# Third combination in the staging tiles, late rows' subtraction tied three products behind their load, last sums made as soon as they are whole

## The chip, the cores and the metric

The kernel runs on one core of one Trainium2 chip. The metric is the device time of one execution in microseconds (us).

## What is computed

The inputs are float32: 2048 rows `x` of width 576, a key and a value cache of 16 heads with 2048 positions, weights, and a conditioning vector `c`. The reference, cut to what matters:

```
mod = silu(c) @ w_mod                      # six vectors of width 576: sa, ca, ga, sb, cb, gb
h = layernorm(x) * (1 + ca) + sa
q = h @ wq                                 # 32 heads of 128; keys/values: 16 heads, last 512 positions
x = x + ga * (softmax(q k^T / sqrt(128)) v) @ wo
h = layernorm(x) * (1 + cb) + sb
x = x + gb * ((sigmoid(h @ w_gate) * (h @ w_up)) @ w_down)     # inner width 4608
```

## The kernel before

**Two stages.** The 2048 rows are four blocks of 512, and a block is four tiles t = 0..3 of 128 rows. Attention runs first, up to about 1801 us. The change touches only the second stage, the gated layer: gate and up products, sigmoid, product, down product.

**Seven products.** Blocks are taken in pairs, pair 0 (blocks 0 and 1) and then pair 1 (blocks 2 and 3, "late rows"). For each pair the step number u runs over 36 slices of the inner width (u = 0..71 in all). A two-by-two matrix product is formed with seven products in place of eight, so each u has seven products A11, A12, S1, S2, S4, S3 and A22 (A22 of u stands behind A11 of u+1). One `product` is seven matmuls (L1087), out of a PSUM tile a, b or c, from a combination `hc` of the pair's normalized rows (seven combinations, c = 0..6) and a weight tile `sw`. Behind each product `load_w` issues one more weight load (L941); ten tiles rotate, so that load stands ten products ahead of its use.

**Combinations.** `combo_parts` makes one combination: 12 transposes on PE (L915) from a staged copy, copies on ScalarE (L918), subtractions on VectorE (L920, L923). In u = 0, product c makes combination c + 2 between its own matmuls. Staged copies come from DRAM (`scr`). For pair 0, combinations 0 to 2 are loaded early into three "rooms" of a large tile, `xp0`. One more is staged in two small tiles tagged "ts" (`stage`, L894). The other three are loaded by `stage_room` (L901) into rooms that have been read: two of them between weight loads 6 and 7 ahead of the first product, one behind the first product. All loads are issued on SyncE (SP in the profile), in order.

**Late rows.** Pair 1's rows are normalized during pair 0. `late_tile(t)` loads two tiles h0, h1 (`h<-xscr`, L1147), subtracts the mean and scales on VectorE (L1152), goes on with GpSimd (L1153, L1154 and three differences), and stores pieces to `scr` (L1161, L1162). It is a generator: `late_some` takes one step behind each product, and pins what the step yields, so it keeps its place in program order. A step that yields `None` only lets one product go by. What is not pinned is placed by a scheduler, which writes each engine's order ahead of time.

**Down products and sums.** `down` makes one of seven partial results (L255, three matmuls into PSUM tile w, of which there are four) and VectorE adds it to an accumulator ACC (L1028; L1026 for the first). 28 downs belong to a group of two u. At the end of a pair, `finish_steps(t)` puts the seven accumulators together: for each t four sums on VectorE (L1011, L1012, L1014, L1016) and four on GpSimd (L1013, L1015, L1017, L1018). The last group of the kernel, GL, is done another way: `open_gl` and `close_gl` (matmuls L1035, L1036, L1043; VectorE L1045) add straight into the four output parts and store them.

In pair 0 the sums stand where the last down of each t is. In pair 1 they wait in a list: before each first down of A11 in the last group four sums are taken from it and pinned (`finish_some(4)`), and one part of the last group goes to `x22`, which the sums read:

```
            if g == GL:
                if a[0] == A11:
                    finish_some(4)
                open_gl(*a, t)
                continue
```

Other VectorE lines named below: L1245 (gate and up for A22), L1282, L1293 (sums ahead of the sigmoids), L1297 and L1300 (v1, ahead of the down products), L977 (low half of `hl`, the down products' left side; its high half is ScalarE's L976).

Of the kernel before, what the change touches and what calls it, by code (L numbers as in the profile page):

```python
# [13 lines left out]
OP = mybir.AluOpType  # L14
# [4 lines left out]
TPB = BLK // P  # L19
# [5 lines left out]
def adaln_block_kernel(ctx: ExitStack, tc: tile.TileContext, x, k_cache, v_cache, wq, wo, w_gate, w_up, w_down,  # L25
                       c, w_mod, out):
    nc = tc.nc
# [53 lines left out]
    def pin(i):  # L81
        tc.keep_in_program_order(i)
# [66 lines left out]
    xp = [const.tile([P, 2, TPB, D], F32, tag=f"xp{h}", name=f"xp{h}") for h in range(2)]  # L149
# [508 lines left out]
    D3 = 3 * P  # L658
# [52 lines left out]
    A11, A12, S1, S2, S4, S3, A22, A21 = range(8)  # L711
# [132 lines left out]
    for n in range(NLO, N + 2 * TPB):  # L844
# [8 lines left out]
        b, i = divmod(n, TPB)  # L853
# [31 lines left out]
    NG = NF // 2  # L885
# [10 lines left out]
        STG[pair, c] = halves  # L896

    def stage_room(c):
        v = xp[0].rearrange("p b t d -> p (b t d)")[:, (c - 3) * TPB * D3 : (c - 2) * TPB * D3]
        v = v.rearrange("p (t d) -> p t d", t=TPB)  # L900
        pin(nc.sync.dma_start(v, scr[0][c]))  # L901
        STG[0, c] = [v[:, 0:2], v[:, 2:4]]
# [46 lines left out]
    ORDER = (A11, S3, A22, S1, A12, S2, S4)  # L949
    WITH = {A11: 0, A12: 1, S1: 2, S2: 3, S4: 6, S3: 4, A22: 5}  # L950
    HL, VAL, SD = {}, {}, {}
    ACC = {}
    for k, a in enumerate(ORDER):
        ACC[a] = bg_view(k // 2, (k % 2) * TPB * D2, [TPB, D2])
    x22 = bg_view(3, TPB * D2, [TPB, D2])

    GL = 2 * NG - 1
# [24 lines left out]
        (nc.gpsimd.tensor_add if op == "+" else nc.gpsimd.tensor_sub)(v, VAL[g, x0], VAL[g, x1])  # L982
        VAL[g, a] = v

    todo, to_finish, X22 = [], [], -1

    def init_acc(pair):
        b0, b1 = 2 * pair, 2 * pair + 1
# [5 lines left out]
        nc.sync.dma_start(of[2 * pair + i][:, t, n0 : n0 + D2], ACC[a][:, t, :])  # L994

    def finish(pair, t):
        for _ in finish_ops(pair, t):
            pass
        if pair == 0:
            for a in (A12, A22, S4, S1):  # L1000
                store_out(a, pair, t)

    def finish_ops(pair, t):
        for i in finish_steps(t):
            if pair:
                pin(i)
            yield i

    def finish_steps(t):
        c = {a: ACC[a][:, t, :] for a in ORDER}  # L1010
        yield nc.vector.tensor_add(c[A12], c[A12], c[A11])  # L1011
        yield nc.vector.tensor_add(c[S2], c[S2], c[A11])  # L1012
        yield nc.gpsimd.tensor_add(c[S4], c[S4], c[S1])  # L1013
        yield nc.vector.tensor_add(c[S3], c[S3], c[S2])  # L1014
        yield nc.gpsimd.tensor_add(c[S1], c[S1], x22[:, t, :])  # L1015
        yield nc.vector.tensor_add(c[A22], c[A22], c[S3])  # L1016
        yield nc.gpsimd.tensor_add(c[S4], c[S4], c[S2])  # L1017
        yield nc.gpsimd.tensor_add(c[S1], c[S1], c[S3])  # L1018

    def down(a, t, hl, w, fresh):  # L1020
        cols = slice(t * P, (t + 1) * P)
# [19 lines left out]
    def close_gl():  # L1041
        p, lo_l, w, val_, to, t = half_done.pop(0)
        nc.tensor.matmul(p, lo_l, w, start=False, stop=True)  # L1043
        acc = x22[:, t, :] if to == X22 else ACC[to][:, t, :]
        nc.vector.tensor_add(acc, p, acc)  # L1045
        if val_ in (A12, A22):
            store_out(to, 1, t)

    def finish_some(k):
        while k and to_finish:  # L1050
            if next(to_finish[0], X22) == X22:
                to_finish.pop(0)
            else:
                k -= 1

    def down_some(k):
        for _ in range(k):
            if not todo:
                return
            g, a, t = todo.pop(0)  # L1060
            if g == GL:
                if a[0] == A11:
                    finish_some(4)
                open_gl(*a, t)
                continue
            down(a, t, HL[g, a], SD[g, a], g % NG == 0 and a in (S3, A11, S1, S2))
            if t == TPB - 1:
                load_sd()
            if a == ORDER[-1] and g == GL - 1:
                to_finish.append(finish_ops(1, t))  # L1070
            elif a == ORDER[-1] and g % NG == NG - 1:
                finish(g // NG, t)

    parts = []
# [67 lines left out]
    def late_tile(t):  # L1142
        lo, hi = slice(0, D2), slice(D2, D)
        h0, h1, ts_ = [fh.tile([P, 2, D3], F32, tag="ts", name=n, bufs=3).rearrange("p a d -> p (a d)")[:, :D]
                       for n in ("h0", "h1", "tt")]
        for i, h in enumerate((h0, h1)):
            nc.sync.dma_start(h, xscr[HB + i][:, t, :])  # L1147
        for _ in range(2):
            yield None
        for i, h in enumerate((h0, h1)):  # L1150
            mv, y = LN[HB + i]
            nc.vector.tensor_scalar(h, h, mv[:, t, 0:1], y[:, t : t + 1], op0=OP.subtract, op1=OP.mult)  # L1152
            yield nc.gpsimd.tensor_mul(h, h, rows2["scale"])  # L1153
            yield nc.gpsimd.tensor_add(h, h, rows2["shift"])  # L1154

        def put(c, v):
            puts.append([2, c, v])

        def put_now(c, v):
            d = scr[1][c][:, t, :]  # L1160
            nc.sync.dma_start(d[:, 0:D2], v)  # L1161
            nc.sync.dma_start(d[:, 2 * P + TQ : 2 * P + 4 * TQ].rearrange("p (q d) -> p q d", q=3),  # L1162
                              v[:, None, 2 * P :].to_broadcast([P, 3, TQ]))

        put_fn[0] = put_now
        put(0, h0[:, lo])
        yield nc.gpsimd.tensor_sub(ts_[:, lo], h1[:, lo], h0[:, lo])
        put(1, h0[:, hi])
        put(2, ts_[:, lo])
        yield nc.gpsimd.tensor_sub(ts_[:, hi], h1[:, hi], ts_[:, lo])  # L1170
        put(3, ts_[:, hi])
        put(4, h1[:, hi])
        yield nc.gpsimd.tensor_sub(h1[:, lo], h1[:, hi], h1[:, lo])
        put(5, h1[:, lo])
        yield nc.gpsimd.tensor_sub(h0[:, lo], h0[:, hi], ts_[:, hi])
        put(6, h0[:, lo])
        for _ in range(4):
            yield None
        assert not puts
# [7 lines left out]

    for c_ in first_ts:
        STG[0, c_] = first_ts[c_]
    stage(0, 6)  # L1190
    for c_ in range(2):
        load_combo(0, c_)
    for n_ in range(10):
        if n_ == 6:
            for c_ in (3, 4):
                stage_room(c_)
        load_w()

# [7 lines left out]
    for u in range(U + 1):  # L1206
# [8 lines left out]
        def swap(c, to):  # L1215
            if u == 0:
                if c == 0:
                    stage_room(5)
                if c in (T2, B22):
                    park_x(HB + c - T2)  # L1220
            if to:
                load_combo(to, c)
                if c + 2 < 7:
                    stage(to, c + 2)
# [8 lines left out]
        if u > 0:  # L1233
            v, qa = back
            g = (u - 1) // 2
            if u == U:
                finish_some(99)
                pd = fpsum("b", 1, [P, BLK])
                product(u - 1, A22, T4, pd, True, (1, 3, 5))
                nc.vector.tensor_add(u3, pd, u3)  # L1240
                nc.vector.tensor_mul(v, u3, v)
            else:
                product(u - 1, A22, T4, qa, False, (1, 3, 5) if u >= U - 1 else (2, 5))
                swap(T4, pair if u % NF == 0 else None)
                nc.vector.tensor_mul(v, qa, v)  # L1245
            if g == GL:
                a, ops = (A11, ((0, A12), (7, S4))) if u % 2 else (A12, ((1, A12), (6, S4)))
                VAL[g, a] = v
                split_val(g, a)
                todo += [(g, (a, o, to), t) for t in range(TPB) for o, to in ops]  # L1250
            elif u % 2:
                VAL[g, A11] = v
                split_val(g, A11)
                sum_val(g, S3, "-", A11, A21)
                later.append((g, S3))
            else:
                VAL[g, A12] = v
                split_val(g, A12)
                sum_val(g, S4, "-", A12, S2)
                later += [(g, a) for a in (S1, S2, S4) if (g, a) not in HL]  # L1260
                if g == GL - 1:
                    split_later()
                    todo += [(g, a, t) for a in ORDER[:2] for t in range(TPB)]
                    todo += [(g, a, t) for t in range(TPB) for a in ORDER[2:]]
                elif g % NG == NG - 1:
                    todo += [(g, a, t) for a in ORDER[:3] for t in range(TPB)]
                    todo += [(g, a, t) for t in range(TPB) for a in ORDER[3:]]
                else:
                    todo += [(g, a, t) for a in ORDER for t in range(TPB)]
# [30 lines left out]
        nc.vector.tensor_mul(v1, v1, g1)  # L1300
        g = u // 2
        if g == GL:
            a, ops = (A22, ((1, A22), (6, S1))) if u % 2 else (A21, ((0, A22), (7, X22)))
            VAL[g, a] = v1
            split_val(g, a)
            todo += [(g, (a, o, to), t) for t in range(TPB) for o, to in ops]
        elif u % 2 == 0:
            VAL[g, A21] = v1
        else:
            VAL[g, A22] = v1  # L1310
            split_val(g, A22)
            sum_val(g, S1, "+", A21, A22)
            if g == GL - 1:
                split_val(g, S1)
            sum_val(g, S2, "-", S1, A11)
            if g == GL - 1:
                split_val(g, S2)
# [29 lines left out]
```

## Time and profile before

| | us |
|---|---|
| median of 3 runs | 3071.37 (3070.59 to 3075.82) |
| the profiled execution's own time | 3071.1 |
| its span in the trace | 3069.3 |
| mean granted TensorE clock | 0.998 |
| PE busy in the span | 3039.1 |

The span is what the trace covers; the time also has 1.8 us around it. PE is busy for 99% of the span. In 40 slices of it PE's busy share is 90% or more in all but the last one, where it is 80 to 90%. Times in microseconds from the span's start place a row in the program: the second stage begins at about 1801, the late rows are normalized up to about 1990, pair 0 ends at about 2450, and the last group of down products begins at about 3030.

### The profile page before, as it was taken

Reading aid. Unit: us, or ns where it says so; the run is one execution under the profiler, and the core shown is the slowest. Engines: PE = TensorE matmul, PEld = TensorE weight load, DVE = VectorE, ACT = ScalarE, POOL = GpSimd, SP = SyncE. Lnnn points to the kernel's source line nnn. Section 1 sums busy time; section 2 is a strip of 40 time slices with the busy share of each in tenths; the row PEclk is TensorE's granted clock in tenths of the full one; section 3 lists DMA queues with packets and bytes.
Section 4 is the critical chain, followed back from the end, with each engine's and each line's share of the span. In section 5 each row is a group of like instructions: output and inputs, shape, how many; then the busy total and the mean of one; then the engine's idle time right before and its main releaser. Section 6 shows DMA issues by size and latency. Waiting matters only on the chain.

```text
span 3069.3 us, 48908 instructions
## 1 busy us (share of the span) xinstructions
PE 3039.1 (99%) x16959; PEld 2635.6 (86%) x16959; DVE 2135.9 (70%) x4145; ACT 1419.7 (46%) x2834; POOL 1487.6 (48%) x1584
## 2 busy tenths in 40 slices
PE   9999999999999999999999999999999999999998
PEld 7888888888888888888888878888888888888887
DVE  7777777777888777777777776555555665555557
ACT  5666656565555555555555543222332323322322
POOL 2656655556334445655555416633444354444433
PEclk9999999999999999999999999999999999999999
DMA  5666766666313346544454458776666676666663
GB/s 165 181 190 177 202 168 170 192 168 190 110 60 96 93 126 163 138 128 134 121 138 127 134 189 267 251 222 197 198 198 199 220 256 198 199 199 198 197 198 109
DMA packets 567841, 526.74 MB, mean 172 GB/s; under 512 B 180518, under 2 KB 443690, under 8 KB 566826
## 3 DMA queue, kind: packets, MB, share of 16 engines
q1 hardware_dynamic: 567584, 523.60, 57.9%
q8 instruction: 135, 2.21, 0.3%
q14 instruction: 112, 0.92, 0.1%
q10 hardware_dynamic: 10, 0.00, 0.0%
HBM read 366.22 MB, written 157.25 MB: 171 GB/s over the span
## 4 chain that ended last, share of the span: by engine, by line
PE 94%; DVE 3%; DMA 2%; issue 0%; ACT 0%; POOL 0%; SPq 0%; DVEq 0%; POOLq 0%; ACTq 0%
PE a L1087 14%; PE wo L255 13%; PE qp L255 13%; PE w L255 12%; PE ot L255 12%; PE st L255 11%; PE st L426 7%; PE c L1087 7%; PE b L1087 4%; PE w L915 1%; DMA h<-xscr 0%; DMA wm<-in_w_mod_dram 0%; DMA sw<-wsc 0%; DVE xp L1014 0%; DMA xp<-scr 0%
## 5 line engine op out<-in xcount | busy, mean ns | idle before, releaser
L1028 DVE TENSOR_TENSOR xp<-w,xp 128x288 f32<-128x288 f32 x948 | 431.8, 457 | 466.2 <-PE w L255 461.2
L255 PE MATMUL wo<-wb,ov 128*128 128x288 f32 x3060 | 615.2, 308 | 0.9 <-DVE ov L444 0.5
L429 ACT ACTIVATE ptt<-st 128x512 fp32r<-128x512 f32 x512 | 306.7, 599 | 635.5 <-PE st L426 635.3
L1087 PE MATMUL a<-hc,sw 128*128 128x512 f32 x2009 | 584.5, 395 | 4.5 <-DVE v L1297 4.4
L255 PEld LDWEIGHTS w<-sd,hl 128*128 128x128 f32 x2940 | 498.3, 188 | 85.2 <-DVE xp L1026 0.9
L459 DVE SCALAR_TENSOR_TENSOR xp<-wo,rs,xp 128x288 f32<-128x288 f32 x1020 | 511.4, 512 | 55.8 <-PE wo L255 6.2
L408 DVE TENSOR_REDUCE neg<-st 128x1 f32<-128x512 f32 x512 | 352.2, 688 | 279.9 <-PE st L255 278.9
L255 PE MATMUL w<-sd,hl 128*128 128x288 f32 x2940 | 546.4, 294 | 0.5 <-DVE xp L1026 0.5
L255 PEld LDWEIGHTS wo<-wb,ov 128*128 128x128 f32 x3060 | 480.4, 189 | 46.6 <-DVE ov L444 0.9
L255 PE MATMUL ot<-ptt,vs 128*128 128x512 f32 x1536 | 441.2, 394 | 0.1
L255 PE MATMUL qp<-hTm,wa 128*128 128x512 f32 x1536 | 438.6, 394 | 1.8 <-DVE qt L388 1.8
L255 PE MATMUL st<-kt,qt 128*128 128x512 f32 x1535 | 434.3, 391 | 0.2 <-DVE ptt L430 0.2
L1087 PEld LDWEIGHTS a<-hc,sw 128*128 128x128 f32 x2009 | 353.3, 188 | 45.5 <-DVE v L1297 6.5
L794 POOL TENSOR_TENSOR xp<-xp 128x896 fp32r<-128x896 f32 (+2 forms) x135 | 260.5, 1929 | 248.8 <-ACT xp L789 246.3
L414 ACT ACTIVATE pp<-st,neg 128x512 f32<-128x512 f32 x512 | 351.3, 686 | 51.3 <-DVE neg L408 49.0
L430 DVE TENSOR_TENSOR ptt<-st,ptt 128x512 fp32r<-128x512 f32 x512 | 348.3, 680 | 4.1 <-ACT ptt L429 3.7
L255 PEld LDWEIGHTS st<-kt,qt 128*128 128x128 f32 x1535 | 287.5, 188 | 60.6 <-DVE ptt L430 0.7
L426 PEld LDWEIGHTS st<-ident,pp 128*128 128x128 f32 x2048 | 253.4, 139 | 67.3 <-ACT pp L414 2.0
L426 PE MATMUL st<-ident,pp 128*128 128x128 f32 x2048 | 306.3, 272 | 0.5 <-ACT pp L414 0.4
L1087 PE MATMUL c<-hc,sw 128*128 128x512 f32 x1008 | 306.3, 395 | 0.1
L255 PEld LDWEIGHTS qp<-hTm,wa 128*128 128x128 f32 x1536 | 260.9, 188 | 27.0 <-DVE qt L388 3.0
L255 PEld LDWEIGHTS ot<-ptt,vs 128*128 128x128 f32 x1536 | 258.7, 188 | 23.0 <-DVE ptt L430 0.3
(198 smaller groups left out, 3562.5 us busy)
## 6 DMA issues: line engine op xcount, KB each, us to landing
sw<-wsc SPq DMA_DIRECT2D x504, 320.0 KB
sd<-dsc SPq DMA_DIRECT2D x249, 288.0 KB
wsc<-xp SPq DMA_DIRECT2D x144, 448.0 KB
dsc<-xp SPq DMA_DIRECT2D x102, 336.0 KB
raw<-in_A_wo_dram SPq DMA_DIRECT2D x64, 288.0 KB
raw<-in_A_wq_dram SPq DMA_DIRECT2D x64, 256.0 KB
wsc<-xp SPq DMA_DIRECT2D x144, 112.0 KB
xp<-in_B_w_gate_dram SPq DMA_DIRECT2D x72, 128.0 KB
```

The source lines that it names most:

```text
L255: nc.tensor.matmul(p, l, r, start=first and n == 0, stop=last and n == len(pairs) - 1)
L408: nc.vector.tensor_reduce(NEG[b][:, i : i + 1], p, axis=AX.X, op=OP.max, negate=True)
L414: keep_order(nc.scalar.activation(PP[n], ST.pop(n), AF.Exp, bias=NEG[b][:, i : i + 1], accum_out=SUM[b][:, i : i + 1]))
L426: nc.tensor.transpose(p[:, k * P : (k + 1) * P], PP[n][:, k * P : (k + 1) * P], ident)
L429: keep_order(nc.scalar.activation(PT[b][:, 0, :, cols], pv_, AF.Copy))
L430: nc.vector.tensor_sub(PT[b][:, 1, :, cols], pv_, f32(PT[b][:, 0, :, cols]))
L459: nc.vector.scalar_tensor_tensor(xv, p, RS[b][:, i : i + 1], xv, op0=OP.mult, op1=OP.add)
L794: pin(nc.gpsimd.tensor_sub(v[:, :n].bitcast(F32R), v[:, :n], hi[:, :n]))
L915: tr = nc.tensor.transpose(p[:, i * P : (i + 1) * P], halves[i // 2][:, i % 2, s * P : (s + 1) * P], ident)
L1028: nc.vector.tensor_add(acc, p, acc)
L1087: mm = nc.tensor.matmul(p, l, r, start=first and n == 0, stop=n == len(pairs) - 1, skip_group_check=not first)
```

## The change

It has three parts.

1. **Start of the second stage.** The two small "ts" tiles stage combination 3 in place of 6, and the rooms take 4, 5 and 6 in place of 3, 4 and 5. Their loads stand where they stood on SP.
2. **Late rows.** Three steps in place of two lie between the loads and the first subtraction, and the subtraction itself is pinned. The scheduler then places the loads otherwise.
3. **The last sums.** The list `to_finish` and `finish_some` are gone. The sums of pair 1 are written right behind the last down of each t of group GL-1, as in pair 0, unpinned; the part that went to `x22` goes to the sum's own accumulator.

```diff
     def stage_room(c):
-        v = xp[0].rearrange("p b t d -> p (b t d)")[:, (c - 3) * TPB * D3 : (c - 2) * TPB * D3]
+        v = xp[0].rearrange("p b t d -> p (b t d)")[:, (c - 4) * TPB * D3 : (c - 3) * TPB * D3]
...
-            if a == ORDER[-1] and g == GL - 1:
-                to_finish.append(finish_ops(1, t))
-            elif a == ORDER[-1] and g % NG == NG - 1:
+            if a == ORDER[-1] and (g % NG == NG - 1 or g == GL - 1):
                 finish(g // NG, t)
...
             if g == GL:
-                if a[0] == A11:
-                    finish_some(4)
                 open_gl(*a, t)
...
-        acc = x22[:, t, :] if to == X22 else ACC[to][:, t, :]
+        acc = ACC[to][:, t, :]
...
-        for _ in range(2):
+        for _ in range(3):
             yield None
         for i, h in enumerate((h0, h1)):
             mv, y = LN[HB + i]
-            nc.vector.tensor_scalar(h, h, mv[:, t, 0:1], y[:, t : t + 1], op0=OP.subtract, op1=OP.mult)
+            pin(nc.vector.tensor_scalar(h, h, mv[:, t, 0:1], y[:, t : t + 1], op0=OP.subtract, op1=OP.mult))
...
-    stage(0, 6)
+    stage(0, 3)
...
-            for c_ in (3, 4):
+            for c_ in (4, 5):
                 stage_room(c_)
...
-                    stage_room(5)
+                    stage_room(6)
...
-                finish_some(99)
                 pd = fpsum("b", 1, [P, BLK])
...
-            a, ops = (A22, ((1, A22), (6, S1))) if u % 2 else (A21, ((0, A22), (7, X22)))
+            a, ops = (A22, ((1, A22), (6, S1))) if u % 2 else (A21, ((0, A22), (7, S1)))
```

Line numbers move: the matmuls of a product are L1067 after, the late loads L1127, the subtraction L1132, v1's sum L1276 and L1279, the sums on VectorE L998, L999, L1001, L1003, the downs' accumulation L1019, the last group's L1036.

The engines' order shows the three places. PE at the start of the second stage, from the first product's last matmul on (a, b, c are the products' PSUM tiles, xp_101 the rooms, ts the small tiles). Before:

```order
L1087 MATMUL a<-hc,sw 128x512
L1087 MATMUL b<-hc,sw 128x512 x2
L915 MATMUL w<-ident,xp_101 128x128 x4
L1087 MATMUL b<-hc,sw 128x512 x2
L915 MATMUL w<-ident,xp_101 128x128 x4
L1087 MATMUL b<-hc,sw 128x512 x2
L915 MATMUL w<-ident,xp_101 128x128 x4
```

After:

```order
L1067 MATMUL a<-hc,sw 128x512
L1067 MATMUL b<-hc,sw 128x512 x2
L915 MATMUL w<-ident,ts 128x128 x4
L1067 MATMUL b<-hc,sw 128x512 x2
L915 MATMUL w<-ident,ts 128x128 x4
L1067 MATMUL b<-hc,sw 128x512 x2
L915 MATMUL w<-ident,ts 128x128 x4
```

The second product now transposes from the small tiles; the rooms are first read again by the third, and the transposes from ts that stood in the fifth product are gone.

VectorE around the second late tile's first subtraction (h is h0, then h1; y_l and mv_l hold its rows' statistics). Before:

```order
L1293 TENSOR_TENSOR g_22017<-c,g_22017 128x512
L1028 TENSOR_TENSOR xp_101<-w,xp_101 128x288
L1152 TENSOR_SCALAR h_22110<-h_22110,mv_l,y_l 128x576
L1028 TENSOR_TENSOR xp_101<-w,xp_101 128x288
L1297 TENSOR_TENSOR v_21983<-a,v_21983 128x512
L1028 TENSOR_TENSOR xp_101<-w,xp_101 128x288
L1300 TENSOR_TENSOR v_21983<-v_21983,g_22017 128x512
```

After:

```order
L1261 TENSOR_TENSOR g_22091<-b,g_22091 128x512
L1019 TENSOR_TENSOR xp_102<-w,xp_102 128x288 x6
L1132 TENSOR_SCALAR h_22137<-h_22137,mv_l,y_l 128x576
L1272 TENSOR_TENSOR g_22191<-c,g_22191 128x512
L1019 TENSOR_TENSOR xp_102<-w,xp_102 128x288 x2
L1276 TENSOR_TENSOR v_22165<-a,v_22165 128x512
L1279 TENSOR_TENSOR v_22165<-v_22165,g_22191 128x512
```

The subtraction moved from behind S4's sum of u = 4 (product 33, counted from 0) to ahead of S4's sum of u = 5 (product 40). On SP its load stands behind weight load 45, that is behind product 35, and no longer behind weight load 42 and product 32. Of the third tile the load stands behind 58 (56 before) and the subtraction still right before L1276, six products later; of the fourth the load stands behind 74 (70 before) and the subtraction behind L1276.

VectorE at the end of the kernel. Before, the first sums stand among the last group's rows (L1045):

```order
L1282 TENSOR_TENSOR g_33742<-b,g_33742 128x512
L1045 TENSOR_TENSOR xp_101<-w,xp_101 128x288
L1045 TENSOR_TENSOR xp_102<-w,xp_102 128x288
L1011 TENSOR_TENSOR xp_102<-xp_102,xp_101 128x288
L1012 TENSOR_TENSOR xp_102<-xp_102,xp_101 128x288
L1045 TENSOR_TENSOR xp_101<-w,xp_101 128x288
L1014 TENSOR_TENSOR xp_101<-xp_101,xp_102 128x288
```

After, they stand among the downs of group GL-1; its last ones, in full:

```order
L1272 TENSOR_TENSOR g_33671<-c,g_33671 128x512
L1003 TENSOR_TENSOR xp_101<-xp_101 128x288
L1019 TENSOR_TENSOR xp_101<-w,xp_101 128x288
L1019 TENSOR_TENSOR xp_102<-w,xp_102 128x288 x3
L998 TENSOR_TENSOR xp_102<-xp_102,xp_101 128x288
L999 TENSOR_TENSOR xp_102<-xp_102,xp_101 128x288
L1276 TENSOR_TENSOR v_33614<-a,v_33614 128x512
L1001 TENSOR_TENSOR xp_101<-xp_101,xp_102 128x288
L1279 TENSOR_TENSOR v_33614<-v_33614,g_33671 128x512
L1003 TENSOR_TENSOR xp_101<-xp_101 128x288
L977 TENSOR_TENSOR hl<-v_33614,hl 128x512
```

All 16 sums now stand ahead of the last group, 14 of them ahead of L1276 and one between L1276 and L1279.

More of the change, by code (lines that the diff above doesn't have):

```diff
@@ L983, in sum_val @@
         VAL[g, a] = v
-    todo, to_finish, X22 = [], [], -1
+    todo = []
     def init_acc(pair):
@@ L996, in finish @@
     def finish(pair, t):
-        for _ in finish_ops(pair, t):
-            pass
+        c = {a: ACC[a][:, t, :] for a in ORDER}
+        nc.vector.tensor_add(c[A12], c[A12], c[A11])
+        nc.vector.tensor_add(c[S2], c[S2], c[A11])
+        nc.gpsimd.tensor_add(c[S4], c[S4], c[S1])
+        nc.vector.tensor_add(c[S3], c[S3], c[S2])
+        nc.gpsimd.tensor_add(c[S1], c[S1], x22[:, t, :])
+        nc.vector.tensor_add(c[A22], c[A22], c[S3])
+        nc.gpsimd.tensor_add(c[S4], c[S4], c[S2])
+        nc.gpsimd.tensor_add(c[S1], c[S1], c[S3])
         if pair == 0:
@@ L1001, in finish @@
                 store_out(a, pair, t)
[L1003 to L1018, printed above, removed]
     def down(a, t, hl, w, fresh):
@@ L1047, in close_gl @@
             store_out(to, 1, t)
[L1049 to L1054, printed above, removed]
     def down_some(k):
```

## The prediction

> **What bounds the kernel.** I read the busy shares first, then the list of what PE waited for, then the timeline at each of those waits. The page's first row and, from PE's waits, the four groups that the change can touch (total us, count, longest):
>
> ```profile
> PE 3039.1 (99%) x16959; PEld 2635.6 (86%) x16959; DVE 2135.9 (70%) x4145; ACT 1419.7 (46%) x2834; POOL 1487.6 (48%) x1584
> ...
> PE w L915 <- DMA xp<-scr: 4.5, 1, 4.5
> PE a L1087 <- DVE v L1297: 4.4, 4, 1.7
> PE w L1035 <- ACT hl L976: 4.3, 1, 4.3
> PE w L1035 <- DVE xp L1045: 3.5, 3, 1.7
> ```
>
> PE is the bound, and it has 3069.3 − 3039.1 = 30.2 us of idle time. The change removes no matmul, so it can win only idle time and time at a lower clock. The four rows hold 16.7 us, and each belongs to one of the three parts; I take the parts one by one.
>
> **Part 1, start of the second stage.** PE's timeline from the second product's first matmuls (start, length, the wait in brackets), and PE's windows with busy time of PE, PEld, DVE, ACT and POOL, granted clock, DMA share, GB/s:
>
> ```profile
> 1807.70 0.63 PE L1087 MATMUL b<-hc,sw 128*128 128x512 f32 x2
> 1812.81 1.09 PE L915 MATMUL w<-ident,xp 128*128 128x128 f32 x4 [4.48 <-DMA xp<-scr]
> ...
> 1821.26 1.79 PE L1087 MATMUL b<-hc,sw 128*128 128x512 f32 x7
> 1822.89 0.60 PE L915 MATMUL w<-ident,xp 128*128 128x128 f32 x4
> ...
> 1825.37 0.63 PE L1087 MATMUL c<-hc,sw 128*128 128x512 f32 x2
> ...
> 1828.33 5.20 PE L1087 MATMUL a<-hc,sw 128*128 128x512 f32 x21
> ```
>
> ```profile
> 1810.00:1812.00 2.00, 0.00 (x0) 0.00 (x0) 0.00 (x0) 0.00 (x0) 0.00 (x0) 0.84 1.03 429
> 1812.00:1814.00 2.00, 1.19 (x5) 1.22 (x6) 0.00 (x0) 0.07 (x1) 0.00 (x0) 0.50 0.98 398
> ...
> 1816.00:1818.00 2.00, 2.00 (x9) 1.60 (x8) 0.92 (x2) 0.87 (x3) 0.00 (x0) 0.50 1.06 416
> ```
>
> From 1807.70 to 1828.33 PE takes 20.63 us for four products with 12 transposes each and a plain one. Undisturbed, the fourth such product took 1828.33 − 1825.37 = 2.96, the plain one (b x7) 1822.89 − 1821.26 = 1.63, together 4 × 2.96 + 1.63 = 13.47. The other 7.16 are the wait of 4.48 and the halved clock behind it. After the change the second product transposes the small tiles, loaded long before. Room 0 is then first needed by the third product: 1807.70 + 2.96 + 0.63 = 1811.29. Its load keeps its place on SP (the rows below, issue time and length), so it lands when it did, and transposes can start at 1812.81: a wait of 1.52 remains.
>
> ```profile
> 1804.81 1.23 SPq L901 DMA_DIRECT2D xp<-scr  x2
> 1806.09 4.26 SPq L941 DMA_DIRECT2D sw<-wsc  x5
> 1810.81 0.32 SPq L901 DMA_DIRECT2D xp<-scr  x1
> ...
> sw<-wsc SPq DMA_DIRECT2D x31, 320.0 KB
> xp<-scr SPq DMA_DIRECT2D x3, 768.0 KB
> ```
>
> Room 2 is now needed two products behind room 0 and with no halved clock between: at about 1812.81 + 2 × 2.96 + 1.63 = 1820.36 with the plain product ahead of it. At 400 GB/s, room 1 (768 KB), five weight tiles and room 2 take 1.9 + 4.0 + 1.9 = 7.8 behind room 0's landing (about 1812.7): 1820.5, a wait of 0.2 to 0.3. The new stretch is 13.47 + 1.52 + 0.25 = 15.25, a gain of 5.4; I take 5.2. Bounds: 7.2 with no wait at all, and 2.5 if the clock halves all the same (7.16 − 4.48 = 2.68 is what that cost before, less any wait that it hides). Why not the lower end: the clock fell in 1810 to 1812 (0.84 is full speed up to about 1811.4 and half from there), some 3 us into a wait of 4.48, and the remaining wait is half of those 3 us. The Trainium skill, "TensorE: Matmul & The Clock Gate", section "What's actually happening", says that the gate goes to half rate after one idle free-running window of about 3.4 us; by that a wait of 1.52 halves nothing and the sum is 5.2 as well, and the rows of 0.84 and 0.50 agree with it.
>
> **Part 2, late rows.** SP's load of the second late tile, VectorE's subtraction and the PE waits behind the second, third and fourth:
>
> ```profile
> 1885.91 0.48 SPq L1147 DMA_DIRECT2D h<-xscr  x1
> ...
> 1891.01 0.58 DVE L1152 TENSOR_SCALAR h<-h,mv_l,y_l 128x576 f32<-128x576 f32 x1 [2.79 <-DMA h<-xscr]
> ...
> 1892.61 0.96 PE L1087 MATMUL a<-hc,sw 128*128 128x512 f32 x3 [1.15 <-DVE v L1297]
> ...
> 1928.30 0.96 PE L1087 MATMUL a<-hc,sw 128*128 128x512 f32 x3 [1.73 <-DVE v L1297]
> ...
> 1963.29 0.96 PE L1087 MATMUL a<-hc,sw 128*128 128x512 f32 x3 [1.02 <-DVE v L1297]
> ```
>
> The load takes 1891.01 − 1885.91 = 5.1 us to land, the subtraction stood a product and a half behind it, and L1297, which frees PE's tile a, stood behind the subtraction. The three waits are 3.90. After, the subtraction stands five, six and five products behind its load. A product with its two downs takes 2.4 to 2.5 us here (from 1892.61 to 1928.30 are two u, 14 products, in 35.69 less the 1.73 wait), so the load has 12 us and more: all 3.90 go. The third tile's subtraction still stands right ahead of L1276; it costs its 0.58 of VectorE there, on PE at most about 0.3 (two such waits of PE's remain short, as the fourth of the group above: 4.4 − 3.90 = 0.5). What else moves: each late tile starts three or four products later and its stores with it. VectorE's other work there is as before; GpSimd's steps move with the tile, and nothing but the stores waits for them. On SP the first store of a tile stands about two products ahead of its value, so the weight loads behind it come some 5 us later; they stand ten products (24 us) ahead of their use and need about 5, which covers it. I take 3.9 (0 to 4.2).
>
> **Part 3, the end.** VectorE and PE in windows over the last 52 us, the last rows of the chain there, and what VectorE's sums took:
>
> ```profile
> 3017.00:3027.00 10.00, 10.00 (x65) 9.22 (x64) 7.45 (x17) 1.25 (x3) 0.81 (x1) 1.00 0.41 116
> 3027.00:3037.00 10.00, 10.00 (x52) 8.10 (x51) 7.10 (x13) 2.38 (x4) 0.81 (x1) 1.00 0.03 11
> 3037.00:3047.00 10.00, 7.06 (x37) 5.25 (x35) 10.00 (x16) 1.20 (x2) 7.02 (x9) 1.00 0.00 0
> 3047.00:3057.00 10.00, 5.13 (x25) 3.91 (x26) 10.00 (x17) 1.86 (x3) 5.01 (x6) 1.00 0.01 2
> 3057.00:3069.30 12.30, 7.66 (x46) 7.24 (x44) 7.49 (x19) 0.63 (x1) 0.00 (x0) 0.79 0.57 193
> ```
>
> ```profile
> 3055.67 0.63 ACT L976 ACTIVATE hl<-v 128x512 fp32r<-128x512 f32 x1 [0.30 <-DVE v L1300]
> 3056.35 0.40 PE L1035 MATMUL w<-sd,hl 128*128 128x288 f32 x1 [4.29 <-ACT hl L976]
> ```
>
> ```profile
> 3037.22 0.45 DVE L1011 TENSOR_TENSOR xp<-xp,xp 128x288 f32<-128x288 f32 x1
> ...
> L1011 DVE TENSOR_TENSOR xp<-xp,xp 128x288 f32<-128x288 f32 x4 | 3.6, 906 | 0.0
> ...
> L1014 DVE TENSOR_TENSOR xp<-xp,xp 128x288 f32<-128x288 f32 x4 | 4.7, 1185 | 0.1
> L1012 DVE TENSOR_TENSOR xp<-xp,xp 128x288 f32<-128x288 f32 x4 | 3.3, 826 | 0.1
> L1011 DVE TENSOR_TENSOR xp<-xp,xp 128x288 f32<-128x288 f32 x4 | 3.0, 760 | 0.1
> L1016 DVE TENSOR_TENSOR xp<-xp 128x288 f32<-128x288 f32 x4 | 2.5, 634 | 0.0
> ```
>
> VectorE is full for 20 us while PE waits 3.47 for L1045 and 4.29 for hl. With the sums out of there VectorE keeps up: 3.47 go, and of the 4.29 some 3.7 (ScalarE's 0.63 stays on the path). The clock of 0.79 behind the long wait costs 0.21 × 12.3 = 2.6 at most; much of that is after PE's last matmul (PE is busy for 7.66 of 12.3), so my estimate is 0.9. Together 8.1. Against that stands what the sums cost in their new place. One sum alone took 0.45 (0.37 from start to start). Beside GpSimd's sums the first group row, of the end, says 0.906; at pair 0's end (the four rows under it), where the sums stood among downs as they now will, (4.7 + 3.3 + 3.0 + 2.5) / 16 = 0.85, less the 0.08 by which neighbours overlap 0.77.
>
> VectorE's first sum follows the ninth of the last 28 downs. The downs come 0.63 apart, and VectorE's other work before L1276 is 17 downs × 0.37 = 6.3, 14 sums, and two ops of 0.6, all behind 3015.94 (the end of the ninth down's accumulation less its overlap):
>
> ```profile
> 3015.57 0.46 DVE L1028 TENSOR_TENSOR xp<-w,xp 128x288 f32<-128x288 f32 x1 [0.17 <-PE w L255]
> ...
> 3026.72 3.19 PE L1087 MATMUL a<-hc,sw 128*128 128x512 f32 x13
> 3029.89 0.40 PE L1035 MATMUL w<-sd,hl 128*128 128x288 f32 x1
> ```
>
> At 0.77 a sum, L1276 ends at 3015.94 + 6.3 + 10.8 + 1.2 = 3034.2; at 0.37 at 3028.6. A22's product adds into tile a, which L1276 reads, and PE's order lets it do only the matmuls before that (like the 13 shown, less A22's) until about 3030.25. It then stands for 4.0. Behind L1276 come a sum (0.77), L1279 (0.6), a hand-over (0.3) and ScalarE's 0.63 before the first open matmul of the last group, 2.3, of which A22's seven matmuls cover 1.6; with the rest and one accumulation that VectorE is behind (0.46), PE loses 4.0 + 0.7 + 0.5 = 5.2. A stand of 4.0 is nearer to the 4.29 and 4.48 behind which the clock fell than to the 1.73 of part 2, so I don't count the clock's 0.9 as won: 8.1 − 0.9 − 5.2 = 2.0. Bounds: with sums at 0.37 L1276 is early and only the 0.5 stays, 7.6. With every sum at 1.1 (1.185 less overlap, the dearest row) L1276 ends at 3038.8, 4.6 later: 2.0 − 4.6 = −2.6, a loss.
>
> **Sum.** 5.2 + 3.9 + 2.0 = 11.1. Against the profiled execution's 3071.1 (span and 1.8 around it) that is 3060.0; the median is 0.27 above that execution, so I say 3060.3.
>
> **Rivals.**
> - *The end wins nothing.* VectorE's backlog only moves ahead, and each sum costs there what it cost at the end: 0.906 and more. L1276 is 14 × 0.14 = 2.0 later still: gain 5.2 + 3.9 + 0 = 9.1, 3062.3. For it: 0.906, and 1.185 for L1014 at pair 0's end. Against it: 0.634 for L1016 there, and VectorE's free time of 2.55 + 2.90 in the two windows from 3017. The Trainium skill, "SBUF — State Buffer", section "Who interferes with whom", says that a VectorE instruction with two SBUF inputs contends with GpSimd's reads, and that the shared port pair is an exclusive lock; that speaks for this rival, and the 0.45 alone against 0.906 agrees with it.
> - *The end wins nearly everything.* Sums come at 0.37, because GpSimd's fall beside downs and not beside VectorE's sums: gain 5.2 + 3.9 + 7.6 = 16.7, 3054.7. For it: 0.45 for the end's first sum. Against it: the means of all five groups.
> - *The clock at the start halves anyway:* gain 2.5 in place of 5.2, 3063.0. Against it: 1.52 is half of what went before the fall.
> - *The subtraction still waits,* because the loads land later than their place in the order says: 3.9 less, 3064.2.
> - *Slower than before.* SP stands at a late tile's store whose value is not there, with the weight loads behind it. It decides from the point where SP stands longer than the weights' lead of ten products less their landing, 24 − 5 = 19 us. To end over 0.2% slower, 11.1 + 6.1 = 17.2 would have to be lost, 4.3 in each of four tiles: SP would have to stand for 23 us, where the order has it stand for two products, 5 us.
>
> **Chances.** Forecast (its own range 3057 to 3062) 0.40, end wins nothing 0.22, end wins nearly everything 0.10, clock at the start 0.08, subtraction waits 0.08. Two of these losses at once, 3065 to 3066, 0.06, and something unnamed that leaves it within 0.2%, 0.03. Slower 0.03. 0.2% is 6.1 us, about what a measurement of this kernel can tell from no change, so down to 3065.2 it is faster: 0.40 + 0.22 + 0.10 + 0.08 + 0.08 = 0.88. The range reaches from the second rival (3054.7, and 3054 where the start's wait is 0.7 shorter than 1.52) to two losses at once (3066), and takes in the largest loss at the end with all else as forecast (3060.3 + 4.6 = 3064.9). It leaves out the slower case and 0.1 or so for terms mis-sized beyond their bounds.
>
> **What would show it.** Start: PE's wait for xp<-scr at 1.5 and 0.3, the granted clock at 1.00 from 1807 to 1824. Late rows: no wait of PE for v, none of VectorE for h<-xscr, no wait for sw. End: a PE wait for L1276 of about 4 to 5 us near 3030, VectorE at 9 or 10 of 10 in the window before, then no wait for L1036's accumulators, and 0.6 to 1 us for the last hl. I would be wrong if PE waits for sw at product 50 and after, if the first wait stays above 3.4 us, or if VectorE is full past L1276 and into the last group.

## The result, and the profile after

| | before | after |
|---|---|---|
| median of 6 runs, us | 3072.57 (3070.16 to 3076.32) | 3054.14 (3053.03 to 3055.38) |
| profiled execution, us | 3071.1 | 3055.38 |
| its span, us | 3069.3 | 3053.3 |

The ratio is 0.9939, 95% interval 0.9926 to 0.9952: 18.4 us faster by the medians (14.7 to 22.7 by the interval). The forecast was 11.1 us, so the direction held and the size did not. The profiled execution after is the slowest of its six.

PE's busy row and the waits that answer to those shown of before, from the page and the list of PE's waits (total us, count, longest):

```profile
PE 3035.3 (99%) x16959; PEld 2632.6 (86%) x16959; DVE 2134.6 (70%) x4145; ACT 1418.4 (46%) x2834; POOL 1491.0 (49%) x1584
...
PE a L1067 <- DVE v L1276: 1.6, 2, 0.8
...
PE w L1026 <- ACT hl L976: 0.9, 2, 0.5
PE w L915 <- DMA xp<-scr: 0.8, 1, 0.8
...
PE w L1026 <- DVE xp L1036: 0.4, 2, 0.3
```

The four groups fell from 16.7 to 3.7 us. PE's busy time fell as well, by 3.8 us, though it issues the same 16959 matmuls: matmuls at half clock take longer and count as busy, and so do the slower matmuls around a wait (0.27 us for each wait, worked out under the late rows below).

The start of the second stage, in PE's timeline and then in two windows with the same columns as before:

```profile
1808.94 0.63 PE L1067 MATMUL b<-hc,sw 128*128 128x512 f32 x2
...
1813.31 0.63 PE L915 MATMUL w<-ident,xp 128*128 128x128 f32 x4 [0.79 <-DMA xp<-scr]
...
1823.74 5.06 PE L1067 MATMUL a<-hc,sw 128*128 128x512 f32 x21
```

```profile
1812.00:1814.00 2.00, 1.21 (x8) 0.77 (x7) 1.94 (x4) 1.97 (x3) 0.00 (x0) 1.00 1.01 385
1816.00:1818.00 2.00, 2.00 (x14) 1.68 (x14) 1.35 (x3) 1.63 (x4) 0.00 (x0) 1.00 1.06 427
```

The stretch is 1823.74 − 1808.94 = 14.80 us in place of 20.63. The wait is 0.79 and not 1.52, and the granted clock stays at 1.00 where it was 0.50.

The second late tile, on SP and VectorE:

```profile
1887.91 0.71 SPq L1127 DMA_DIRECT2D h<-xscr  x1
...
1898.95 0.57 DVE L1132 TENSOR_SCALAR h<-h,mv_l,y_l 128x576 f32<-128x576 f32 x1
```

The load has 1898.95 − 1887.91 = 11.0 us and the subtraction no longer waits. PE has no wait for v between 1840 and 1990.

The end, in windows, and VectorE's sums there (busy, mean ns):

```profile
3007.00:3017.00 10.00, 9.91 (x61) 8.53 (x60) 9.96 (x21) 0.85 (x2) 8.20 (x9) 1.00 0.34 92
3017.00:3027.00 10.00, 8.52 (x41) 6.28 (x40) 10.00 (x19) 2.36 (x4) 6.90 (x7) 1.00 0.11 34
3027.00:3037.00 10.00, 10.00 (x58) 8.88 (x58) 6.39 (x15) 1.85 (x4) 0.00 (x0) 1.00 0.00 0
3037.00:3047.00 10.00, 9.05 (x55) 7.70 (x54) 9.22 (x21) 2.49 (x4) 0.00 (x0) 1.00 0.27 90
```

```profile
L999 DVE TENSOR_TENSOR xp<-xp,xp 128x288 f32<-128x288 f32 x4 | 3.6, 909 | 0.0
L1003 DVE TENSOR_TENSOR xp<-xp 128x288 f32<-128x288 f32 x4 | 2.9, 724 | 0.0
L998 DVE TENSOR_TENSOR xp<-xp,xp 128x288 f32<-128x288 f32 x4 | 2.4, 601 | 0.0
L1001 DVE TENSOR_TENSOR xp<-xp,xp 128x288 f32<-128x288 f32 x4 | 2.3, 566 | 0.0
```

VectorE is full from 3007 to 3027, as the prediction had it, but it reaches L1276 some 2 us earlier than forecast: a sum took on average (3.6 + 2.9 + 2.4 + 2.3) / 16 = 0.70, or 0.62 from start to start. The stand at L1276:

```profile
3021.92 0.68 DVE L1276 TENSOR_TENSOR v<-a,v 128x512 f32<-128x512 f32 x1
...
3020.49 1.33 PE L1067 MATMUL b<-hc,sw 128*128 128x512 f32 x5
3022.65 1.90 PE L1067 MATMUL a<-hc,sw 128*128 128x512 f32 x7 [0.83 <-DVE v L1276]
...
3040.92 0.40 PE L1026 MATMUL w<-sd,hl 128*128 128x288 f32 x1 [0.52 <-ACT hl L976]
```

PE stands for 0.83 us where 4.0 was forecast, and for 0.52 at the last hl where it stood for 4.29. One sign that the prediction gave for being wrong did come: VectorE is still full up to 3027, while the last group begins at 3024.9 (L1026, behind a wait of 0.35 for hl). It cost little: PE's waits for the last group's accumulators are 0.4 us in all.

To see where the time went, I set the two traces side by side at the same down product (the n-th matmul of L255 into tile w, 2940 in each trace). Before, the points are at 1801.05 (attention's last matmul into tile wo), 1843.86 (first down), 1990.64, 2404.63, 2490.07, 3006.52 and the span's end. How much later or earlier the other trace goes through each stretch, in us:

| trace | attention | start | late rows | rest of pair 0 | change of pairs | pair 1 | end | sum |
|---|---|---|---|---|---|---|---|---|
| after | +1.24 | −5.97 | −4.79 | −1.13 | +0.87 | 0.00 | −6.19 | −15.96 |
| part 1 alone | +1.01 | −6.34 | +2.08 | −0.01 | +2.19 | 0.00 | +0.51 | −0.54 |
| part 2 alone | +0.12 | −1.97 | −4.79 | −1.14 | +0.08 | 0.00 | −0.55 | −8.25 |
| part 3 alone | +0.55 | −0.64 | +2.96 | 0.00 | −0.30 | 0.00 | −6.20 | −3.62 |
| after, sums all on VectorE | +0.05 | −6.19 | −4.79 | −1.13 | +0.66 | 0.00 | −2.94 | −14.35 |
| after, sums all on GpSimd | −0.30 | −3.36 | −4.79 | −1.14 | −1.07 | 0.00 | −2.89 | −13.54 |
| after, two steps pinned | +1.31 | −5.61 | −4.79 | −1.13 | +0.11 | 0.00 | −6.16 | −16.27 |
| after, three steps unpinned | +1.71 | −5.64 | −1.86 | −1.13 | −0.35 | 0.00 | −6.20 | −13.47 |
| before, sums all on VectorE | −0.21 | −1.59 | +3.48 | −0.01 | −0.88 | 0.00 | −1.49 | −0.68 |
| after, rooms earlier and last t later | +0.52 | −5.33 | −4.79 | −1.14 | −0.32 | 0.00 | −5.74 | −16.80 |
| after, two steps and room 2 early | −0.14 | −6.71 | −4.39 | 0.00 | +0.02 | 0.00 | −6.16 | −17.38 |

The +1.24 in attention has nothing to do with the change. It is one stretch of half clock near 22 us in the traced execution of after, in this row of its windows; before has 1.00 there, behind the same wait of 1.41 us for L535:

```profile
22.00:25.50 3.50, 3.50 (x16) 3.21 (x16) 2.95 (x5) 3.25 (x7) 0.00 (x0) 0.52 0.99 346
```

Without it the traces differ by 17.2 us; the medians say 18.4.

### The profile page after: what moved, and what is told of

The parts are those of the page before. It is cut to its first block, busy times and chain, and to the rows that moved or that the text cites. A ratio compares the mean times of both kernels' runs of the same rounds, so it can differ in the third digit from the quotient of the medians.

```text
span 3053.3 us, 48907 instructions
## 1 busy us (share of the span) xinstructions
PE 3035.3 (99%) x16959; PEld 2632.6 (86%) x16959; DVE 2134.6 (70%) x4145; ACT 1418.4 (46%) x2834; POOL 1491.0 (49%) x1584
## 4 chain that ended last, share of the span: by engine, by line
PE 96%; DVE 3%; DMA 1%; issue 0%; ACT 0%; SPq 0%; POOL 0%; DVEq 0%; ACTq 0%; POOLq 0%
PE a L1067 15%; PE qp L255 13%; PE wo L255 13%; PE w L255 12%; PE ot L255 12%; PE st L255 11%; PE c L1067 7%; PE st L426 7%; PE b L1067 4%; PE w L915 0%; DVE xp L1019 0%; DMA wm<-in_w_mod_dram 0%; DMA xp<-scr 0%; PE st L283 0%; DVE xp L999 0%
## 5 line engine op out<-in xcount | busy, mean ns | idle before, releaser
L1019 DVE TENSOR_TENSOR xp<-w,xp 128x288 f32<-128x288 f32 x948 | 430.4, 456 | 463.6 <-PE w L255 460.0
L255 PE MATMUL wo<-wb,ov 128*128 128x288 f32 x3060 | 615.3, 308 | 0.9 <-DVE ov L444 0.5
L1067 PE MATMUL a<-hc,sw 128*128 128x512 f32 x2009 | 583.1, 395 | 1.7 <-DVE v L1276 1.6
L255 PEld LDWEIGHTS w<-sd,hl 128*128 128x128 f32 x2940 | 496.7, 188 | 87.0 <-DVE xp L1019 1.8
L255 PE MATMUL w<-sd,hl 128*128 128x288 f32 x2940 | 545.9, 294 | 0.8 <-DVE xp L1017 0.5
L255 PEld LDWEIGHTS wo<-wb,ov 128*128 128x128 f32 x3060 | 480.4, 189 | 46.5 <-DVE ov L444 0.9
L255 PE MATMUL ot<-ptt,vs 128*128 128x512 f32 x1536 | 441.2, 394 | 0.1
L255 PE MATMUL qp<-hTm,wa 128*128 128x512 f32 x1536 | 439.3, 394 | 1.6 <-DVE qt L388 1.6
L255 PE MATMUL st<-kt,qt 128*128 128x512 f32 x1535 | 434.2, 391 | 0.2 <-DVE ptt L430 0.2
L1067 PEld LDWEIGHTS a<-hc,sw 128*128 128x128 f32 x2009 | 353.7, 188 | 41.7 <-DVE v L1276 2.8
L255 PEld LDWEIGHTS st<-kt,qt 128*128 128x128 f32 x1535 | 287.4, 188 | 60.7 <-DVE ptt L430 0.7
L1067 PE MATMUL c<-hc,sw 128*128 128x512 f32 x1008 | 306.0, 395 | 0.1
L255 PEld LDWEIGHTS qp<-hTm,wa 128*128 128x128 f32 x1536 | 261.4, 188 | 26.9 <-DVE qt L388 2.8
L255 PEld LDWEIGHTS ot<-ptt,vs 128*128 128x128 f32 x1536 | 258.9, 188 | 22.9 <-DVE ptt L430 0.3
```

What stands on the lines that cost most here:

```text
L255: nc.tensor.matmul(p, l, r, start=first and n == 0, stop=last and n == len(pairs) - 1)
L1067: mm = nc.tensor.matmul(p, l, r, start=first and n == 0, stop=n == len(pairs) - 1, skip_group_check=not first)
```

## The experiments

My theory after the result: three separate gains, each the waits that it removes and the clock behind them, and at the end a sum on VectorE costs 0.37 us by itself and what GpSimd's operations beside it add. The rivals: the parts help only together, and the price of a sum belongs to its place in the order.

**Each part alone, on the kernel before.** Part 1 is, with the room numbers that follow from it,

```diff
-    stage(0, 6)
+    stage(0, 3)
-            for c_ in (3, 4):
+            for c_ in (4, 5):
-                    stage_room(5)
+                    stage_room(6)
```

part 2 the third step and the pin,

```diff
-        for _ in range(2):
+        for _ in range(3):
-            nc.vector.tensor_scalar(h, h, mv[:, t, 0:1], y[:, t : t + 1], op0=OP.subtract, op1=OP.mult)
+            pin(nc.vector.tensor_scalar(h, h, mv[:, t, 0:1], y[:, t : t + 1], op0=OP.subtract, op1=OP.mult))
```

and part 3 the rest of the change:

```diff
-                if a[0] == A11:
-                    finish_some(4)
...
-            elif a == ORDER[-1] and g % NG == NG - 1:
+            if a == ORDER[-1] and (g % NG == NG - 1 or g == GL - 1):
```

> Part 1 alone on the kernel before. Theory (three separate gains, each equal to the waits that it takes away and the clock behind them): PE's stretch from the second product to the plain run of 21 matmuls goes from 20.6 to 14.8 us as in the changed kernel, the late rows' three waits (3.9) and the end's (3.5 and 4.3) stay; the time falls by 5 to 7 us. Rival (the parts work only together, for instance because an earlier start only lets PE run into a later wait): it falls by less than 3 us and a wait grows somewhere behind 1830 us.

> Part 2 alone on the kernel before. Theory: PE's three waits for v (3.9) go and with them the slower first matmuls behind them; 4 to 5 us less, nothing else moves. Rival (the wait only moves to a product a little later, or to the staged tiles at the change of pairs): less than 2 us, and a new wait of PE between 1890 and 2000 us or near 2400 us.

> Part 3 alone on the kernel before. Theory: the stand at v1's last but one sum is under 1 us, the waits of 3.5 and 4.3 go; 6 to 7 us less. Rival (the prediction's own working: a stand of 4.0 there, when the kernel's clock history is as before): about 2 us less.

Measured: 3065.98 (ratio 0.9981, 0.9972 to 0.9990), 3066.65 (0.9977, 0.9968 to 0.9986) and 3065.88 (0.9975, 0.9966 to 0.9985), against 3073.0 for the kernel before in 25 runs. By the medians the three are 7.0, 6.4 and 7.1 us, together 20.5, where all at once give 18.4; by the ratios 5.8, 7.1 and 7.7, that is 0.0067 against 0.0061. Each part helps alone, so the rival that they help only together is out, and the gains add up within the intervals, which are wide: some 6 us more or less would not show. Part 1 came as expected, part 3 at or just above the upper edge, and part 2 above the 4 to 5 us that I expected.

The table gives each changed stretch alike: −6.34 against −5.97 at the start, −4.79 in both for the late rows, −6.20 against −6.19 at the end. A stretch that was not changed moves too, so one trace of before is no firm base: the kernels with the old start have −0.64 to −1.97 there, and the other three with the old late rows (part 1 alone, part 3 alone, before with its sums on VectorE) +2.08 to +3.48. Each of these three has 3.4 us of half clock in the late rows, and before's trace has none. In such executions part 2 is worth 7 to 8 us and not 4.8, which would fit its median.

PE's waits of part 3 alone still show the two other parts' waits, and the stand at L1276 is the same 0.8 (0.82 at 3035.0; three more of this row's five are the late rows'):

```profile
PE a L1067 <- DVE v L1276: 6.2, 5, 2.1
PE w L915 <- DMA xp<-scr: 4.7, 1, 4.7
```

The sums of the rows in the table are far smaller than these medians for parts 1 and 3 (−0.54, −3.62). The profiled execution of part 1 alone is the slowest of its 11 (3070.84); besides the late rows' half clock it has a wait of 2.04 us for L1297 at the change of pairs.

**The price of a sum: all sums of pair 1 on VectorE.**

```diff
-        nc.gpsimd.tensor_add(c[S4], c[S4], c[S1])
+        add(c[S4], c[S4], c[S1])          # add: VectorE for pair 1, GpSimd for pair 0; so too the other three
```

> The changed kernel with all eight sums of each t of pair 1 on VectorE, so none beside GpSimd. Theory (a sum's price is 0.37 from start to start and what is above it is GpSimd's): 28 sums stand before v1's last but one sum at 0.37 to 0.45 each in place of 14 at 0.62, which ends about 2 to 3 us later; 1.5 to 3 us slower than the changed kernel. Rival (the price is that of the place, among the downs, whoever shares it): 28 at 0.62, 8 to 9 us slower than the changed kernel.

> The kernel before, its sums in their old place in the last group, with all 32 of pair 1 on VectorE. Theory (a sum costs 0.37 without GpSimd beside it): 32 x 0.37 = 11.8 us of VectorE in place of 16 x 0.82 = 13.1, so the last v1 is 1.3 us earlier: 1 to 2 us faster than before. Rival (0.82 is the price of the place): 26 us, 13 us slower.

Measured: after with it 3056.71 (3055.18 to 3057.32), 2.6 slower than after's median (1.5 by the ratios, 0.9944 against 0.9939, whose intervals overlap), so the 8 to 9 us of the rival are out; before with it 3070.38, ratio 0.9992 (0.9983 to 1.0001), which is no measurable change but excludes 13 us. Two rows of VectorE's groups, a sum that was on VectorE and one that came from GpSimd, first of after with it, then of before with it:

```profile
L1000 DVE TENSOR_TENSOR xp<-xp,xp 128x288 f32<-128x288 f32 x4 | 1.8, 457 | 0.0
L1005 DVE TENSOR_TENSOR xp<-xp 128x288 f32<-128x288 f32 x4 | 1.8, 456 | 0.0
```

```profile
L1013 DVE TENSOR_TENSOR xp<-xp,xp 128x288 f32<-128x288 f32 x4 | 1.8, 453 | 0.0
L1018 DVE TENSOR_TENSOR xp<-xp 128x288 f32<-128x288 f32 x4 | 1.8, 454 | 0.0
```

In both places a sum takes 0.45 (0.37 from start to start) when GpSimd does none, and L999's 0.909 falls to L1000's 0.457 for the same instruction. The price above 0.45 comes with GpSimd's sums, not with the place. Twice as many sums at 0.37 take longer than half of them at 0.62, so PE's stand grew, and the granted clock was 0.50 from 3024 to 3030 behind it:

```profile
PE a L1068 <- DVE v L1277: 3.1, 1, 3.1
```

**The other extreme: all sums of pair 1 on GpSimd** (the same edit the other way).

```diff
-        nc.vector.tensor_add(c[A12], c[A12], c[A11])
+        add(c[A12], c[A12], c[A11])       # add: GpSimd for pair 1, VectorE for pair 0; so too the other three
```

> The changed kernel with all eight sums of each t of pair 1 on GpSimd, none on VectorE. Theory (what PE waits for is VectorE's queue ahead of v1's sum, and GpSimd's 32 x 0.8 = 25 us lie beside it from 3006 to 3031 us): no stand at v1's sum, 1 us faster at the end than the changed kernel, unless the last t's accumulations wait for GpSimd. Rival (GpSimd's reads slow VectorE's other work, or the last group waits for the sums): the same or slower than the changed kernel, with VectorE waiting for xp of GpSimd near 3030 us.

Measured: 3055.28 (3054.19 to 3057.52), 1.1 slower than after's median; the end alone gained 2.89 in place of 6.19 (the table). The rival came out, as far as this trace tells. The stand at v1's sum is gone, and the last group waits for GpSimd instead, VectorE's accumulation first and PE behind it:

```profile
DVE xp L1037 <- POOL xp L1004: 2.9, 1, 2.9
DVE xp L1037 <- POOL xp L1006: 1.8, 1, 1.8
```

```profile
PE w L1027 <- DVE xp L1037: 3.1, 4, 1.5
```

Here too the clock was at 0.50 (from 3032 to 3038, behind the first of these waits), which is part of the 3 us. In the traces the half and half of the change is the best of the three splits: from 3007 to 3027 VectorE is full and GpSimd busy for 15.1 of 20 us (the windows above). The times alone don't settle it: the ratios are 0.9939, 0.9944 and 0.9946, with intervals that overlap.

**The late rows: distance or pin.** After with two steps and the pin, and with three steps and no pin.

```diff
-        for _ in range(3):
+        for _ in range(2):
```

```diff
-            pin(nc.vector.tensor_scalar(h, h, mv[:, t, 0:1], y[:, t : t + 1], op0=OP.subtract, op1=OP.mult))
+            nc.vector.tensor_scalar(h, h, mv[:, t, 0:1], y[:, t : t + 1], op0=OP.subtract, op1=OP.mult)
```

> The changed kernel with two steps in place of three between the late loads and the subtraction, the subtraction pinned. In the order the subtractions of tiles 2 to 4 now stand four products behind their load, all ahead of S4's sum. Theory (what counts is that the load has more than its 5.1 us to land; a product takes 2.4): no wait of PE for v, 3053 to 3055, as the changed kernel. Rival (the third step is what takes the wait away): waits of 1 us and more come back, 3057 or more.

> The changed kernel with the three steps but the subtraction not pinned. The scheduler then writes the subtractions of tiles 2 and 3 one product behind their loads, behind v1's product with the gate. Theory (distance decides): VectorE waits for h<-xscr 2 to 3 us at each of the two, PE is held for 1 to 3 us in all, 3056 to 3058. Rival (three steps alone do it): no wait, 3054.

Measured: 3052.30 (3051.94 to 3054.78) and 3056.93 (3056.05 to 3057.59), two ranges that don't touch. The theory holds: with the pin two steps are enough, and the third step alone is not. Without the pin VectorE waits again, longer than I expected (12.2 us in four waits):

```profile
DVE h L1132 <- DMA h<-xscr: 12.2, 4, 5.1
```

PE's listed waits there are only 1.3, and the stretch as a whole is 2.9 longer than in after (the table). Matmul by matmul, 2.6 of it stand at three places, near 1929, 1933 and 1968, in waits of 1.09, 0.13 and 0.21 and in the slower matmuls around them. The pin is what carries part 2.

**Two attempts at a still faster kernel.** Both start from after. The first loads rooms 0 and 1 two weight tiles earlier and writes the last t's sums only when the last group's turn comes. The second has two pinned steps at the late rows, rooms 0 and 1 behind four weight loads, and room 2 ahead of three of the ten.

```diff
-        if n_ == 6:
+        if n_ == 4:
             for c_ in (4, 5):
                 stage_room(c_)
...
+            if a == ORDER[-1] and g == GL - 1 and t == TPB - 1:
+                last_t.append(t)              # finish(1, t) when the last group's turn comes
```

```diff
-    for n_ in range(10):
-        if n_ == 6:
+    for n_ in range(7):
+        if n_ == 4:
...
                     stage_room(6)
+                    for _ in range(3):
+                        load_w()
```

> The changed kernel with two more edits: the loads of rooms 0 and 1 stand behind four weight loads in place of six, and the last t's sums are written behind the first matmul of the last group, so v1's last but one sum is ahead of them. Theory: the start's wait of 0.8 goes (two tiles of 0.8 us less ahead of the room), the stand of 0.83 and the 0.35 behind it go: 1.5 to 2.5 us faster than the changed kernel. Rival (SP stands at the rooms, which are still being read, and the weights behind them come late; or the sums now hold the last group's accumulations): the same or slower, with a PE wait for sw or for L1036.

> The changed kernel with two pinned steps at the late rows, rooms 0 and 1 behind four weight loads and room 2 behind eight in place of eleven (three weight loads moved behind it). Theory (the start's wait is the place in one queue of all that stands ahead of the last room): both waits at the start, 0.8 to 1 us with room 2's, go, and the late rows' 0.8 too: 1.5 to 2 us faster than the changed kernel, 3052 to 3053. Rival (weight tiles come late): a PE wait for sw between 1815 and 1840 us.

Measured: 3054.48 (3051.21 to 3057.49) and 3053.67 (3051.76 to 3056.59). Neither differs from after's 3054.14. In the first the wait for room 0 went, and room 2's took its place, since the same weight tiles and rooms still stand ahead of it on SP and PE is there earlier; the table has the start at −5.33, no better than −5.97. The end was no better either (−5.74): PE waited 0.41 at v1's sum and 0.56 for hl. In the second, with three weight tiles moved behind room 2, the start's wait for the rooms is halved, a gain of 0.7 in the trace that the medians cannot show. The wait for rooms, first of the one, then of the other:

```profile
PE w L915 <- DMA xp<-scr: 1.8, 1, 1.8
```

```profile
PE w L915 <- DMA xp<-scr: 0.4, 1, 0.4
```

Of all versions run, the two pinned steps have the lowest median (3052.30, ratio 0.9932, 0.9919 to 0.9946). It is below both kernels, but its runs overlap those of after.

## Why the prediction was right and wrong

- **Start, forecast 5.2, measured 5.97.** Right, with luck in the size. The wait is 0.79 and not 1.52 since this execution reaches the room's first transpose 1.2 us later, after its slow stretch at 22 us, while the room landed 0.5 later. At room 2 PE waited 0.19, near the 0.25 forecast. The trace names VectorE's L1095 for it, but in the trace with all sums on GpSimd the same transposes start at 1822.32 while that instruction runs until 1822.57, so they don't need it; what is left is the room's load. In after's trace the clock did not fall, so the third rival did not come there. It did come in the trace with all sums on GpSimd, whose start is the same and which was there earlier: PE waited 2.18 for the first room (the trace names VectorE's L1096, but in after that instruction runs only behind these transposes), the clock fell to half, and the gain was 3.36:

```profile
1813.17 1.09 PE L915 MATMUL w<-ident,xp 128*128 128x128 f32 x4 [2.18 <-DVE st L1096]
```

```profile
1814.00:1816.00 2.00, 2.00 (x9) 1.70 (x8) 0.69 (x1) 0.60 (x1) 0.00 (x0) 0.50 1.04 407
```

- **Late rows, forecast 3.9, measured 4.79.** The mechanism was right, all three waits went; the size lies above my bound of 4.2. The 0.9 more is what a wait costs besides its listed length. In a run of these matmuls (128x512) one starts every 0.23 us, and each one's record is 0.40 long. A wait is counted from the end of the record ahead of it, so 0.40 − 0.23 = 0.17 is lost there, and behind the wait the second matmul starts 0.33 after the first and not 0.23. That is 0.27 for each wait, 0.8 for three. What part 2 had put at nothing is the clock: in before's trace it did not fall at the late rows, in the three other traces with the old late rows it did (the experiments). The third tile's subtraction ahead of L1276 cost PE no wait that shows. The fourth rival did not come, nor did the slower one: PE has no wait for sw anywhere among its listed waits.
- **The end, forecast 2.0, measured 6.19: this is the step that failed.** The gross gain of 8.1 was near: the waits of 3.47 and 4.29 fell to 0.4 and 0.5, and the clock behind the long one was worth 1.7 and not 0.9 (it was 0.50 from 3057.3 to 3060.6, with PE at work until 3064.7). The loss was mis-sized: "PE loses 4.0 + 0.7 + 0.5 = 5.2", most of it the stand at L1276, "It then stands for 4.0". PE stood for 0.83 there. Two terms of the 4.0 were off. The sums came at 0.62 from start to start and not 0.77, which brings the end of L1276 1.8 us earlier (from 3024.4, the forecast's 3034.2 moved by the 9.8 us that the trace is ahead there, to 3022.6). And PE got there 1.3 us later than I had it (3021.8 against 3030.25 − 9.8), held at the downs before by the same VectorE, as a listed wait of 0.30 for L1019 at 3017.7 shows; the rest is in downs that start later than before. This delay shortens the stand but is lost all the same: with it, the 0.83 and the 0.35 for hl the loss is about 2.5 in place of 5.2, and 8.1 + 0.8 for the clock − 2.5 = 6.4 is what PE gained (the stores behind PE's last matmul took 0.2 longer). I took the price from pair 0's end as the nearest row, where the four groups mean 0.85; here the mean is 0.70. Downs' accumulations stand between the sums in both places. What differs in the traces is GpSimd: at pair 0's end it also has other operations of 1.4 to 1.5 us and is idle for 0.8 us beside VectorE's sums, here it does nothing but its own sums and is idle for 3.7. With the stand short the clock stayed at 1.00 until PE's last matmul, so the clock's share was won too, which I had written off on the strength of a stand of 4.0 that did not come. That such a stand costs it is borne out by the run with all sums on VectorE: a stand of 3.1, and half clock behind it.
- **The rivals.** The end's second rival, 16.7 us in all, came nearest to the total, but not by its mechanism: sums did not come at 0.37. The first rival's mechanism, sums made dearer by GpSimd's, is shown by the two kernels without it (0.45 for every sum), and its price was smaller than I feared. That rival's 2.0 was also too dear by its own row: it set 0.906, a mean length, against 0.77, which is from start to start; like against like the difference is 0.06 a sum, 0.8 us for 14.
- **What no step had.** PE went through pair 0 after the late rows 1.13 us faster, with no wait in either trace, and the change of pairs 0.87 us slower, where its waits for staged copies (`ts<-scr`, `rows_ss<-scr`) grew from 0.22 to 0.66 and the one for v1's sum from 0.50 to 0.74. And the baseline: before's median is 3072.57 in six runs, 1.2 above the three I had.

## What to carry to other kernels

Waits of PE add up to more than their lengths: each cost some 0.27 us more here, and some brought a stretch at half clock. Where one engine's operations slow another's (a sum on VectorE took 0.45 us without GpSimd's sums and up to 1.06 beside them), neither the price of an operation alone nor that in another place carries over: it depends on what the other engine does just then. In these traces an even split, with other work between the sums, beat giving all of them to either engine. To keep a consumer behind its load, pin the consumer: a distance in steps alone is undone by the scheduler.

## What the runs showed of the hardware

Waits of about 2 us can halve the clock. I had compared a wait of 4.48 (clock fell) with one of 1.73 in the late rows (it did not). In part 3 alone, a wait of 2.07 in the same place as the 1.73 was enough. Windows of that trace:

```profile
1926.50:1930.00 3.50, 1.43 (x9) 0.96 (x7) 2.40 (x5) 0.60 (x1) 0.00 (x0) 1.00 0.99 356
1930.00:1933.50 3.50, 3.50 (x12) 3.04 (x11) 1.96 (x6) 0.00 (x0) 0.00 (x0) 0.51 0.11 42
```

PE was busy for 1.43 of 3.5 us, and the next 3.5 us ran at half clock. The Trainium skill, "TensorE: Matmul & The Clock Gate", section "What's actually happening", names an idle window of about 3.4 us as the condition; here a window that was 59% idle did it, so the measurement decides against reading it as fully idle. In part 1 alone the wait at the same place was 3.16 and the clock fell as well (0.60 in the window behind it). Whether the clock falls differs between executions with the same waits: at the end of the kernel before, waits of 1.68 and 1.49 kept it at 1.00 in before's trace, and the same two were followed by half clock in that of part 2 alone (from 3040.9). That may be why the kernel before spreads over 6.2 us in the six runs of the first table and after over 2.4: before's trace has seven waits of PE of 1 to 4.5 us in the places of the change. It is not shown, and one variant speaks against it: after with rooms earlier and last t later spread over 6.3 us in five runs, and its trace has only one wait over 1 us in these places.

It stays open why PE takes about 1.13 us less for the rest of pair 0 in after, in part 2 alone and in five variants of after, and not in the variant with room 2 early, nor in any kernel without part 2: the matmuls and their order are the same, and no wait shows.
